# One order of work for four engines and two queues, written out by hand and drawn up anew

## The chip, the cores and the metric

The kernel runs on one core of one Trainium2 chip. The core has TensorE (PE; its weight loads are listed as PEld), VectorE (DVE), ScalarE (ACT), GpSimd (POOL) and SyncE (SP). Each of them works through its own instructions in the order in which they were emitted. SyncE and GpSimd issue the DMA transfers of this kernel, each through a queue of its own (q1 and q0 on the profile's page). The metric is the device time of one execution in microseconds (us).

## The reference

Two independent layers over a sequence of S = 2048 with D = 1024 channels, bf16; their results stand side by side in the output.

```python
# A: a short shift convolution (4 taps), a long convolution by FFT of length 2S, two gates
k_shift = sum over t of k_pad[:, t:t + S, :] * shift_k[:, ks - 1 - t]
kv = k_shift * v
y = irfft(rfft(kv padded to 2S) * rfft(ssm_k padded to 2S))[:S]
a = q * (y + kv * ssm_D)
# B: a diagonal state space layer with 1024 complex states
Bu = einsum("bld,pd->blp", x, B_bar)
h[t] = Lam_bar * h[t - 1] + Bu[t]
b = 2.0 * einsum("blp,dp->bld", hseq, Cmat).real + x * Dskip
return concatenate([a, b], -1)
```

## The kernel before

**The order is a string.** The whole kernel is emitted by one loop over the words of `ORDER` (L67 to L186, 1489 words). A word names a task, its arguments and the slots that it takes: `lh.15:a41` calls the function that `E` holds under `lh` with the argument 15 and gives it unit 41. `p` is one of 8 PSUM banks, `a` one of 53 units of 1024 elements a partition in one SBUF buffer (the arena; a task of several units takes neighbouring ones from the number on), `h` one of 3 slots for the scans' results (gslot), `w` one of 3 slots for constant matrices (wslot). The functions (L268 to L765) emit one task each. Since every engine and queue works in order of emission, the sequence of the words is the sequence of work on each of them. Where two tasks touch the same bytes of a slot, the later one waits for the earlier: a load into a unit waits until the last reader of that unit is done, also where this reader is a store that is still under way, and what stands behind the load on its queue waits with it.

**Layer A** is an FFT in two stages, both done by matrix products.

- `kp`, `vp` (L570 to L579) load rows of k and v; `kvm`, `kva`, `kvb`, `kvc` (L588 to L603, VectorE) do the shift convolution and the product with v.
- `am` (L608) is the first stage for kv, `ae` (L614) evicts it, `ast` (L617, GpSimd) stores it to a scratch in HBM. `hl` (L623) loads the long filter, `hT` (L632) transposes it on TensorE, `hc` and `hd` (L637 to L647) evict it, `hm` (L657), `he` (L665) and `hst` (L668) are its first stage.
- For each of 16 pairs of frequency groups, `lw` (L672) loads the pair's constant matrix into a wslot, `lh` and `lk` (L677) load the scratch rows of filter and kv, `sh` and `sk` (L688) are the second stage, `she` (L697) and `ske` (L704) evict it, `sw` (L708, GpSimd) or `swp` (L708, SyncE) swaps partitions by a transfer, `pr` (L714, VectorE) multiplies the spectra, `sa` (L726) is the way back, `sae` (L734) evicts it and `vst` (L737, GpSimd) stores it.
- `vl` (L742) loads that in the other order, `qp` (L747) loads q, `a3` (L754) is the last stage, `a3e` (L761) evicts it, `qm` (VectorE) multiplies by q, and `ost` (L764, GpSimd) or `osp` (L765, SyncE) stores the output.

**Layer B** runs in 16 blocks of 128 steps.

- The head: small tables of the parameters (`ld_par`, `par_T` L279, `p32` L284, `dve2`, `sin0` and others), `wb` and `wbe` (L402, L408) for the shift taps; `bl`, `bT`, `bc` (L415 to L431) load, transpose and evict B; `cl`, `cT`, `cx`, `cc` (L435 to L439) do the same for C; `dd` (L371, VectorE) makes diagonal matrices of Dskip.
- Each block: `x` (L447, SyncE) loads x transposed, `U` (L464) multiplies it by B, `ue` (L473) evicts, `r1` and `r3` (L487), `r2` (L498), `cy` (L500), `sc` (L504, the scan itself) and `r4` (L510) are VectorE's and ScalarE's part, `y` (L520, L523) or `yq` (L538) multiplies by C, `ye` (L556) evicts, and `ysh`, `ysp` (SyncE), `ysg`, `yst` (GpSimd) store (L560 to L564).

An eviction is a copy from PSUM. Its word without a `v` is ScalarE's, with a `v` (`a3ev`, `saev`, `bcv`) VectorE's:

```python
    def either(nm, f):
        E[nm] = lambda *a: f(nc.scalar.copy, *a)
        E[nm + "v"] = lambda *a: f(nc.vector.tensor_copy, *a)
```

Of the kernel before, what the change touches and what calls it, by code (L numbers as in the profile page):

```python
# [72 lines left out]
bT.2.1:p0 U.0.0.1 bT.3.0:p7 bc.5.0 bc.2.1 bc.5.1 kva.3 kring U.1.2.0:p5 bl.3.1:a23 cl.0.0:a14 bT.2.0:p2 bT.3.1:p0
bl.7.1:a46 ue.1.0:a34 U.0.2.1:p6 bc.3.1 bc.2.0 U.0.2.0 U.1.2.1 cl.3.0:a37 bl.7.0:a26 cl.1.0:a25 bT.7.1:p2 kvb.3:a22
bT.7.0:p0 ue.0.0:a23 bc.6.1 kp.-2 x.3:a21 U.0.1.0:p3 bc.3.0 gz stt cl.2.0:a12 cT.0.0:p4 bc.7.0 bc.7.1 U.0.1.1 U.0.3.0:p0
kvm.1:a15 ue.1.2 vp.1:a27 U.0.3.1 U.3.2.0:p1 ue.0.1 U.3.0.0:p3 z1 kvm.2:a42 z2 ld_Q U.1.1.1:p2 ue.0.2 ue.0.3 x.2:a52
U.1.1.0 cl.3.1:a13 kva.1 cT.1.0:p7 cl.2.1:a32 kva.2 kvb.1:a14 kvb.2:a39 ue.1.1 kvm.0:a15 rta kvc.3 U.3.0.1 cx.6.0 kva.0
cc.1.0 am.3.1:p0p6 cl.1.1:a51 U.3.1.1:p2 ue.3.0:a44 ae.3.0.1:a19 cc.0.0 U.3.2.1 kvc.2 ue.3.2 am.3.0:p7p3 cT.3.1:p0
vp.0:a30 cc.3.1 cx.7.0 kvb.0:a29 U.3.1.0 ue.3.1 cT.1.1:p5 U.3.3.0:p4 r1.0:a46 ae.3.1.1 kvc.0 U.3.3.1 kp.2 am.2.1:p2p0
r2.0:h1 cc.1.1 ue.3.3 cl.0.1:a27 hl.0.1:a23 kvc.1 am.0.0:p5p6 ae.3.0.0 cT.2.1:p1 ae.2.1.1:a40 sc.0.0 hl.0.0 U.1.3.1:p4  # L80
ae.3.1.0 sc.0.1 U.1.3.0 am.0.1:p3p0 ae.0.1.0:a31 cc.2.1 ae.0.0.0 ae.0.0.1 ae.0.1.1 ae.2.0.1 cT.0.1:p7 U.2.0.1:p1
r1.3:a15 cc.0.1 ue.1.3 ast.0 U.2.0.0 am.1.1:p5p3 r3.0:a27 cx.5.0 U.2.3.0:p0 ae.1.0.1:a46 hl.1.0:a48 hl.1.1 ae.1.1.1
# [5 lines left out]
he.0.7.0.0:a50 y.0.0.3 hc.0.0:a13 hm.0.6.0:p4p2 ye.0.0:a19 hm.0.4.1:p5p7 y.0.1.0:p6 y.0.1.1 y.0.1.2 y.0.1.3 vp.2:a34
kvb.4:a31 he.0.6.0.0 sc.1.1 he.0.4.1.1 vp.3:a26 r1.2:a14 he.0.4.1.0 he.0.7.0.1 hst.0.7.0 r3.1:a46 hm.0.0.1:p1p5
hst.0.4.1 hc.0.5:a42 he.0.6.0.1 r4.1 hm.0.0.0:p2p3 he.0.0.1.0:a48 cy.2:h1 r2.2 hm.0.5.1:p7p0 ye.0.1 he.0.5.1.1:a23  # L90
he.0.5.1.0 kp.3 he.0.0.1.1 kvm.6:a38 he.0.0.0.0 y.1.1.0:p4 kvc.4 y.1.1.1 hst.0.6.0 hst.0.6.1 kp.4 kva.6 hst.0.5.1
hm.0.5.0:p6p0 he.0.5.0.0 kvm.5:a14 y.1.1.2 he.0.0.0.1 kvb.6:a25 he.0.5.0.1 y.1.1.3 hm.0.7.1:p2p7 ye.1.1:a28 he.0.7.1.0
# [5 lines left out]
kvb.7:a31 ysp.0 U.4.0.1 r3.2:a48 hT.1.6:p5 he.0.1.1.1 ast.6 ast.4 he.0.2.1.0 hT.1.5:p4 r4.2 he.0.2.0.1 kvc.7 hT.1.4:p6
U.4.2.1:p1 ue.4.1 ue.4.0 hc.1.6:a22 hc.1.4:a19 am.5.1:p7p0 hT.1.3:p2 U.4.2.0 hc.1.5:a33 hT.1.7:p3 am.5.0:p6p4
ae.5.0.1:a15 yst.1 cy.3 y.2.1.0:p7 kp.5 hT.1.1:p5 hst.0.2.0 hd.2 y.2.1.1 ae.5.1.0 hdv.3 ae.5.0.0 hc.1.7:a30 ae.5.1.1  # L100
hst.0.2.1 hT.1.2:p4 y.2.0.0:p6 ue.4.2 hc.1.1:a14 sc.3.1 sc.3.0 hT.1.0:p0 y.2.0.1 am.7.0:p3p1 hc.1.3:a18 hst.0.1.0
r3.3:a40 hm.1.7.1:p5p2 hc.1.0:a34 ae.7.1.0:a27 he.1.7.1.1:a25 hst.0.3.0 y.2.1.2 ae.7.0.0 hst.0.3.1 am.7.1:p2p1 ast.5
# [6 lines left out]
hm.1.5.1:p2p6 he.1.5.1.1:a51 he.1.5.1.0 hst.1.5.1 yq.3.6 yq.3.7 ye.3.1:a24 hm.1.5.0:p6p4 kvm.11:a28 he.1.2.0.1 hst.1.2.0  # L109
hm.1.0.1:p3p5 cy.4 he.1.5.0.0 kp.6 kvb.10:a33 U.5.1.1:p2 U.5.1.0 sc.4.0 U.6.3.0:p7 kva.11 sc.4.1 hst.1.3.1 ye.3.0  # L110
ue.5.1:a40 he.1.0.1.0:a17 U.5.3.1:p2 hm.1.0.0:p3p1 kvc.9 ast.8 he.1.5.0.1 hst.1.5.0 kvb.11:a46 hm.1.6.0:p0p6 he.1.0.0.0
he.1.0.0.1 he.1.6.0.1:a47 U.5.3.0 hst.1.2.1 hst.1.3.0 U.6.3.1 he.1.6.0.0 U.6.0.1:p1 hm.1.1.0:p6p0 ue.5.3 ysp.3
hm.1.1.1:p2p3 he.1.0.1.1 hm.1.6.1:p5p4 he.1.1.0.0:a22 U.6.0.0 r3.4:a42 he.1.6.1.0 kvm.13:a12 he.1.1.1.1 U.5.2.0:p6
ue.6.0 U.5.2.1 he.1.6.1.1 hst.1.6.1 r4.4 he.1.1.1.0 hst.1.1.1 U.7.0.0:p3 he.1.1.0.1 vp.5:a50 U.5.0.0:p0 hst.1.0.1
hst.1.0.0 kvc.10 am.9.0:p2p4 kvc.11 kva.13 U.7.0.1 ae.9.1.0:a29 kvm.15:a49 ae.9.0.0 ue.7.0:a24 U.5.0.1 U.7.3.0:p4 ue.5.0
am.9.1:p1p0 vp.7:a34 ae.9.0.1 x.10:a26 kvb.13:a17 U.7.3.1 vp.6:a42 am.10.0:p3p1 kvm.14:a18 kvm.12:a13 kva.15 yq.4.0:p5p2
yq.4.1 yq.4.2 yq.4.3 ae.10.0.0:a44 ae.10.1.0 ue.7.3 ae.9.1.1 am.11.1:p3p0 ue.5.2 U.7.1.0:p1 kvc.13 ue.6.3 am.10.1:p4p6
ae.10.1.1 hst.1.1.0 kva.12 U.7.1.1 kvb.15:a4 am.11.0:p6p7 cy.5:h1 yq.4.4 kva.14 kvc.15 ae.10.0.1 yq.4.5 ue.7.1 yq.4.6
yq.4.7 kvb.14:a32 x.8:a23 ae.11.0.1:a10 ae.11.1.1 hst.1.6.0 lh.0:a46 ae.11.1.0 ae.11.0.0 ye.4.0:a28 am.13.0:p3p1
am.13.1:p6p0 ye.4.1 ae.13.0.1:a48 ae.13.0.0 U.6.2.0:p7 lh.1:a8 U.6.2.1 U.7.2.1:p4 am.15.0:p6p2 ast.9 x.9:a52 kvb.12:a50  # L120
ae.13.1.0 ue.6.2 ae.13.1.1 ae.15.0.0:a19 U.7.2.0 kvc.14 ae.15.1.0 am.14.0:p7p3 ue.7.2 ae.14.0.0:a29 ae.14.1.0
am.15.1:p6p1 am.14.1:p2p5 ae.15.0.1 U.8.3.0:p7 ast.10 lw.0:w0 ast.13 r1.5:a15 kvc.12 am.12.0:p4p3 ast.11 r2.5 ae.14.0.1
# [720 lines left out]
```

## Time and profile before

| | before |
| --- | --- |
| device time, median of 3 runs | 343.81 us (343.48 to 343.87) |
| profiled execution, its span | 343.2 us |
| TensorE matmuls busy | 329.5 us |
| VectorE busy | 325.1 us |
| ScalarE busy | 273.5 us |
| GpSimd busy | 68.9 us |
| moved by DMA | 100.83 MB |

The profile is of one execution. Its span runs from the first to the last recorded instruction; the device time is a little longer. "Busy" is the time in which an engine works on an instruction that the profile counts; issuing transfers, waiting on semaphores and branching are not counted. A line of waits tells who sat idle, until what came; a row of the timeline tells the start, the duration, the engine, the line of the kernel, the operation with its tiles and, in brackets, the idle time before it. A DMA's row on SPq or POOL is its issue only; when it has landed stands in a row of its own.

### The profile page before, as it was taken

The numbers are of one execution on the slowest core, as the hardware profiler recorded it, in microseconds if no ns is written. First come the engines' busy times: TensorE is split into PE (matmuls) and PEld (weight loads), VectorE is DVE, ScalarE is ACT, GpSimd is POOL, SyncE is SP. The second block draws the span as 40 slices with busy tenths as digits, with TensorE's granted clock in tenths as the row PEclk, the third lists the DMA queues.
The fourth block names the chain that finished last, engine by engine and source line by source line (L and its number), as shares of the span: only waits on it lengthen the run. The fifth ranks groups of instructions, "written<-read, shape, count | busy, mean of one in ns | idle before, by whom it ended". The sixth has DMA issues, their size and how long they took to land.

```text
span 343.2 us, 11813 instructions
## 1 busy us (share of the span) xinstructions
PE 329.5 (96%) x5086; PEld 230.2 (67%) x5105; DVE 325.1 (95%) x263; ACT 273.5 (80%) x519; POOL 68.9 (20%) x111
## 2 busy tenths in 40 slices
PE   5799999999999999999999999999999999999993
...
DVE  4989999999999999999999999999989999999991
...
PEclk9999999999999999999999999999999999999998
...
GB/s 177 352 351 208 315 281 283 155 318 365 368 269 198 264 263 295 233 261 343 313 353 282 270 339 212 369 272 311 280 314 276 216 326 378 327 335 284 375 346 274
DMA packets 62592, 100.83 MB, mean 294 GB/s; under 512 B 29422, under 2 KB 31614, under 8 KB 62540
## 3 DMA queue, kind: packets, MB, share of 16 engines
...
## 4 chain that ended last, share of the span: by engine, by line
PE 74%; ACT 15%; DMA 4%; issue 3%; DVE 3%; SPq 0%; POOL 0%; DVEq 0%; POOLq 0%
PE bank L464 25%; PE bank L538 19%; PE bank L520 10%; PE bank L754 4%; PE bank L688 4%; PE bank L726 4%; PE bank L608 2%; PE bank L657 2%; ACT BT L431 2%; ACT arena L614 2%; ACT arena L473 2%; ACT CT L439 2%; ACT arena L637 2%; DMA wslot<-a_c_W 1%; DMA arena<-arena 1%
## 5 line engine op out<-in xcount | busy, mean ns | idle before, releaser
L464 PEld LDWEIGHTS <-BT 128*128 128x128 bf16 x2048 | 117.8, 98 | 14.4 <-issue 9.9
L464 PE MATMUL bank<-arena,BT 128*128 128x128 bf16 x2048 | 125.4, 221 | 1.1 <-ACT BT L431 0.9
L538 PE MATMUL bank<-CT,gslot 64*64 64x512 bf16 x1408 | 86.6, 378 | 0.0
L504 DVE TENSOR_TENSOR_SCAN gslot<-rtab,gslot 128x1040 bf16<-128x1040 f32 x32 | 73.0, 2311 | 0.5
L538 PEld LDWEIGHTS <-gslot 64*64 64x64 bf16 x1408 | 36.9, 107 | 30.8 <-issue 1.9
L473 ACT CAST arena<-bank 128x512 bf16<-128x512 f32 x63 | 40.5, 660 | 13.8 <-PE bank L464 13.4
L614 ACT CAST arena<-bank 128x512 bf16<-128x512 f32 x64 | 37.2, 680 | 6.7 <-PE bank L608 4.0
L697 ACT CAST arena<-bank 128x512 bf16<-128x512 f32 x63 | 35.0, 617 | 5.9 <-issue 2.8
L520 PE MATMUL bank<-CT,gslot 128*128 128x512 bf16 x153 | 38.5, 380 | 0.3
L665 ACT CAST arena<-bank 128x512 bf16<-128x512 f32 x64 | 35.2, 631 | 3.1 <-PE bank L657 3.0
L714 DVE TENSOR_TENSOR arena<-arena 128x4096 bf16<-128x4096 bf16 x16 | 36.5, 2280 | 1.1 <-DMA arena<-arena 1.0
L487 DVE TENSOR_TENSOR arena<-gslot,Z 128x4096 bf16<-128x4096 bf16 x16 | 36.6, 2287 | 0.8 <-DVE gslot L504 0.2
L704 ACT CAST arena<-bank 128x512 bf16<-128x512 f32 x60 | 34.4, 621 | 3.2 <-PE bank L688 3.0
L734 ACT CAST arena<-bank 128x512 bf16<-128x512 f32 x60 | 32.4, 616 | 5.5 <-PE bank L726 5.3
L487 DVE TENSOR_TENSOR arena<-arena,Z 128x4096 bf16<-128x4096 bf16 x16 | 36.5, 2280 | 0.1
L556 ACT CAST arena<-bank 128x512 bf16<-128x512 f32 x31 | 18.1, 599 | 16.6 <-PE bank L538 8.7
L588 DVE TENSOR_TENSOR arena<-arena 128x4096 bf16<-128x4096 bf16 (+3 forms) x16 | 30.0, 1881 | 0.0
L668 POOL DMA_DIRECT2D Ys_h<-arena x32 | 23.2, 735 | 25.5 <-ACT arena L665 20.2
L617 POOL DMA_DIRECT2D Ys_kv<-arena x16 | 11.2, 726 | 83.5 <-ACT arena L614 81.1
L520 PEld LDWEIGHTS <-gslot 128*128 128x128 bf16 x160 | 14.1, 98 | 15.9 <-issue 2.3
L688 PE MATMUL bank<-arena,wslot 64*64 64x512 bf16 x256 | 21.5, 382 | 0.3 <-DMA wslot<-a_c_W 0.3
L737 POOL DMA_DIRECT2D Vs<-arena x16 | 11.7, 731 | 46.3 <-ACT arena L734 41.3
...
## 6 DMA issues: line engine op xcount, KB each, us to landing
Ys_kv<-arena POOLq DMA_DIRECT2D x16, 512.0 KB, 5.6
...
arena<-Ys_h SPq DMA_DIRECT2D x16, 512.0 KB, 5.0
arena<-Ys_kv SPq DMA_DIRECT2D x16, 512.0 KB, 5.6
Vs<-arena POOLq DMA_DIRECT2D x16, 512.0 KB, 5.6
arena<-Vs SPq DMA_DIRECT2D x16, 512.0 KB, 6.7
...
arena<-in_A_k_dram SPq DMA_DIRECT2D x8, 512.0 KB, 5.2
```

What stands on the lines that cost most here:

```text
L464: nc.tensor.matmul(pu[:, w, jl, :], BT[:, 2 * jp + jl, w, d, :], xT[:, d, :], start=(d == 0), stop=(d == ND - 1))
L473: cp(st["u", i][:, :, 2 * jp:2 * jp + 2, :], st.pop(("pu", i, jp)))
L487: nc.vector.tensor_mul(m, s_, win(Z))
L504: nc.vector.tensor_tensor_scan(gf, rtab[:].rearrange("p j t -> p (j t)"), gf, 0.0, ALU.mult, ALU.add)
L520: nc.tensor.matmul(py, h[:, w, j, 2:GW], CT[:, j, w, dh * 512:(dh + 1) * 512], start=(j == 0 and w == 0), stop=False)
L538: mm = nc.tensor.matmul(st["py", i, dh][cols, cs(r)], lhs(dh, rows, c), rhs(dh, rows), start=first, stop=last)
L614: cp(st["ysb", n2][:, p, dh * 512:(dh + 1) * 512], st.pop(("pa", n2, p, dh)))
L665: cp(o, st.pop(("pb", hf, s, e, r)).rearrange("p (n c t) -> p n c t", n=2, c=2))
L688: nc.tensor.matmul(st["ps", nm, g, l][64 * dh:64 * dh + 64, :], st["w", i][rows, a * WC:a * WC + 64], st[nm, i][rows, a, dh * 512:(dh + 1) ...
L697: cp(st["hab", i][:, 0, a, l, :], st.pop(("ps", "h", g, l)))
L704: cp(st["x16", i][:, a, l, :], st.pop(("ps", "k", g, l)))
L714: nc.vector.tensor_mul(hab, st.pop(("x16", i)).rearrange("p a l d -> p (a l d)").unsqueeze(1).to_broadcast([P, 2, 2 * D]), hab)
```

## The change

Only `ORDER` is changed; every function stays. The string after holds the same 1489 words up to the engine letters, so the same work.

- Compute tasks come in another sequence, and nearly all slots have other numbers.
- The loads and stores on SyncE and GpSimd keep their sequence, but for the stores that change queue: `ysp.4`, `ysp.6`, `ysp.10`, `ysp.13` and `osp.7` go to GpSimd as `yst` and `ost`; `yst.5`, `yst.11`, `ysg.14.0`, `ysg.15.1` and `ost.1` go to SyncE as `ysp`, `ysh` and `osp`. `ld_Q` comes ahead of `gz`.
- Evictions that change engine: VectorE's `a3ev` go from 9 to 6, `saev` from 4 to 2, `skev` from 4 to 3, `shev` and `uev` from 1 to 2 each; VectorE evicts 16 tiles in place of 20.

The string's lines that matter below, of 120 on either side: the head, the lines with `hl.2.1`, `x.5` and `lh.15`, and the tail.

```diff
-ld_w:a22 wb.3:p3 ld_par wbe.3:a8 par_T:p4 wb.0:p5 wb.7:p1 p32 ld_F bl.1.0:a39 bl.0.1:a18 wb.5:p7 bl.6.0:a34 bl.4.1:a14
-exp1 dve2 wbe.0 dve3 wb.6:p2 wb.4:p3 wb.2:p0 sm_pre wbe.7 bl.0.0:a27 wbe.5 x.0:a38 wb.1:p7 wbe.6 exp2 kp.1:a0 bl.1.1:a21
...
-he.0.3.1.0:a36 kvc.6 y.1.0.1 he.0.3.1.1 hst.0.5.0 kvb.5:a12 sc.2.1 ae.4.1.0 he.0.3.0.1 kvm.7:a13 y.1.0.2 am.4.1:p1p7
-hl.3.0:a40 he.0.3.0.0 hm.0.1.0:p5p0 y.1.0.3 he.0.1.0.0:a38 am.6.1:p5p6 ae.4.1.1 U.4.3.1:p7 he.0.1.0.1 ae.6.0.1:a17
-hl.2.1:a44 U.4.3.0 kvc.5 ae.6.1.1 am.6.0:p6p5 U.4.0.0:p2 ae.4.0.1 ue.4.3:a23 U.4.1.1:p3 ae.6.0.0 hm.0.2.0:p0p6 ae.6.1.0
...
-hst.1.7.0 he.1.3.1.1 yq.3.3 hm.1.2.1:p7p6 x.6:a37 he.1.2.1.0:a19 kva.9 he.1.2.1.1 he.1.3.0.0 kvc.8 x.5:a36 lw.1:w2
-kvb.9:a35 kvm.10:a47 U.6.1.0:p3 U.6.1.1 am.8.1:p6p7 ast.7 hst.1.7.1 r1.4:a40 kva.10 ae.8.1.1:a44 hst.1.4.1 ae.8.0.1
-r2.4:h0 am.8.0:p5p2 ae.8.0.0 ae.8.1.0 hst.1.4.0 ue.6.1:a38 yq.3.4 yq.3.5 hm.1.2.0:p5p7 he.1.2.0.0 x.7:a27 kp.7
...
-ske.22.1 yq.10.1 yq.10.2 ske.18.0 sw.9.0 vst.8 ye.9.0 sa.15:p6p5 lh.15:a41 ske.23.0 cy.11:h0 pr.9 ske.23.1 sae.15.1:a50
-x.12:a52 swp.11.0 r1.11:a20 yq.10.3 sa.14:p7p3 sae.15.0 sae.14.0 sa.19:p5p4 lw.10:w0 sa.18:p6p1 lk.12:a16 r2.11 yq.10.4
-sae.18.0:a39 yq.10.5 sae.19.0 saev.19.1 sae.14.1 vst.7 yq.10.6 yq.10.7 sh.20:p6p7 sh.21:p3p4 she.20.0:a3 sae.18.1
...
-a3.7.1:p6 a3e.7.1 a3.7.0:p4 a3e.7.0 qm.2 qm.0 osp.0 osp.2 yst.12 a3e.15.1 a3.6.1:p3 a3ev.6.1 qm.3 y.15.1.1 y.15.1.2
-y.15.1.3 ysg.14.1 ost.3 ye.15.1:a1 ysg.15.1 y.15.0.0:p4 y.15.0.1 a3e.15.0 y.15.0.2 qm.7 osp.7 y.15.0.3 ye.15.0 ysh.15.0
+ld_w:a33 ld_par par_T:p1 p32 dd exp1 dve2 wb.5:p0 wbe.5:a8 wb.7:p1 wbe.7 ld_F wb.0:p2 wbe.0 dve3 tabA1:a40a50a47a29
+bl.1.0:a32 wb.4:p7 wbe.4 wb.1:p4 wbe.1 bT.1.0:p3 bc.1.0 wb.3:p5 bl.0.1:a12 sm_pre bl.6.0:a26 bl.4.1:a39 bl.0.0:a24
...
+ae.6.1.1 hm.0.1.1:p4p1 r4.2 he.0.1.1.0 he.0.1.1.1 U.4.0.0 hl.3.0:a39 hl.2.1:a44 kvc.7 U.4.1.0:p3 hst.0.7.1 hl.3.1 hl.2.0
...
+he.1.2.1.1 am.8.1:p3p2 ae.8.0.1:a12 he.1.3.1.1 am.8.0:p5p4 ae.8.1.0 ae.8.0.0 ae.8.1.1 kvb.9:a19 U.6.1.1 r1.4:a39 x.5:a36
...
+sae.15.0:a39 sae.15.1 sa.14:p7p1 sae.14.0 sa.19:p6p3 sae.19.1:a15 sa.18:p5p4 sae.18.0 yq.10.4 yq.10.5 yq.10.6 yq.10.7
+sae.14.1 sae.18.1 vst.8 lh.15:a42 x.12:a47 swp.11.0 pr.11 ye.10.0:a49 lw.10:w0 sh.20:p1p7 she.20.1:a32 sh.21:p4p5
...
+y.15.1.0:p7 y.15.1.1 y.15.1.2 y.15.1.3 y.15.0.2 y.15.0.3 ye.15.1:a38 ye.15.0 ysh.14.0 qp.3:a32 a3ev.7.0 qm.3 ost.5 qm.2
+osp.4 osp.1 osp.0 osp.2 yst.12 ysg.14.1 ost.3 ysh.15.1 qm.7 ost.7 ysh.15.0
```

Unit 44 in the new string is taken by `kvm.2` at the head and later by others, the last reader ahead of `hl.2.1` being `kvb.5`; unit 36's last reader ahead of `x.5` is `am.8.0`; unit 42 ahead of `lh.15` holds the result that `vst.8` stores.

More of the change, by code (lines that the diff above doesn't have):

```diff
@@ L73 @@
[L73 to L82, printed above, removed]
@@ L88 @@
[L88 to L92, printed above, removed]
@@ L98 @@
[L98 to L102, printed above, removed]
@@ L108 @@
-r2.4:h0 am.8.0:p5p2 ae.8.0.0 ae.8.1.0 hst.1.4.0 ue.6.1:a38 yq.3.4 yq.3.5 hm.1.2.0:p5p7 he.1.2.0.0 x.7:a27 kp.7
[L109 to L122, printed above, removed]
@@ L133 @@
-sh.5:p0p3 she.5.0:a32 yq.6.2 yst.5 she.4.1 yq.6.3 lw.5:w1 sk.5:p0p5 she.4.0 she.5.1 sa.1:p4p2 sa.0:p1p3 ske.5.0:a13
-sae.1.0:a8 yq.6.4 ske.5.1 sae.0.0 sae.1.1 yq.6.5 sae.0.1 sh.10:p4p5 she.10.1:a0 she.10.0 yq.6.6 sh.11:p5p0 she.11.0
-she.11.1 yq.6.7 swp.2.0 sk.4:p1p4 ske.4.1 r3.7:a42 r4.7 yq.7.0:p5p2 yq.7.1 ye.6.1:a21 lw.4:w0 sw.5.1 ske.4.0 ye.6.0
-x.14:a36 swp.2.1 cy.8:h2 sh.9:p3p0 yq.7.2 she.9.0:a48 sh.8:p7p1 lk.7:a46 swp.5.0 yq.7.3 vst.0 she.9.1 r1.8:a4 she.8.1
-she.8.0 lk.4:a40 sk.11:p0p3 ysp.6 ske.11.1:a28 sk.10:p4p6 pr.2 sa.5:p7p1 ske.10.0 ske.11.0 yq.7.4 ske.10.1 sa.4:p4p3
@@ L143 @@
-ske.12.0 x.11:a14 lk.8:a12 r2.9 yq.8.5 r1.10:a41 sh.17:p7p2 yst.7 sh.16:p4p6 vst.4 lh.7:a32 swp.6.0 yq.8.6 yq.8.7 vst.5
-sc.9.0 she.17.1:a6 sk.17:p2p3 she.16.0 she.16.1 sk.13:p5p6 swp.6.1 she.17.0 ye.8.1:a25 ye.8.0 U.11.0.1:p4 sc.9.1
-r3.9:a48 ske.13.1 U.11.0.0 ske.17.1:a16 ske.13.0 ue.11.0:a18 pr.6 sk.16:p7p0 lw.7:w0 sh.15:p1p6 sw.8.1 U.11.3.1:p5
-U.11.3.0 ske.16.1 she.15.1:a37 ske.17.0 she.15.0 sk.15:p2p0 sh.14:p3p6 ysp.8 ue.11.3 r4.9 U.11.1.1:p1 ske.16.0 U.11.1.0
-ske.15.0:a12 she.14.1 sa.12:p2p6 ske.15.1 she.14.0 swp.8.0 x.13:a31 sa.13:p0p4 ue.11.1 U.11.2.0:p7 cy.10:h2 sk.14:p3p1
@@ new lines @@
+wb.6:p0 wbe.6 x.0:a38 wb.2:p6 kp.1:a0 bT.0.1:p2 wbe.3 wbe.2 bc.0.1 bT.0.0:p0 bc.0.0 bl.1.1:a31 tabA2 exp2 sin0 par_rest
+sin1 kp.0 bT.6.0:p7 x.1:a33 kvm.3:a17 bT.4.1:p1 U.0.0.0:p6 bT.1.1:p0 bl.3.0:a42 sin2 eo bT.3.0:p3 bc.3.0 bl.5.1:a36
+bT.5.1:p4 bl.2.1:a45 bl.4.0:a32 bl.6.1:a12 U.1.0.0:p2 bc.4.1 bT.4.0:p5 bc.4.0 bl.5.0:a31 bl.2.0:a14 bcv.1.1 U.1.0.1
+ue.1.0:a34 kva.3 kp.-1 bT.2.0:p0 bc.5.1 bcv.6.0 bT.5.0:p7 bc.5.0 bl.3.1:a36 cl.0.0:a37 bT.2.1:p1 bc.2.1 kring bc.2.0
+kvb.3:a42 stt kvm.1:a15 kvm.2:a44 bl.7.1:a43 cl.3.0:a20 U.1.2.0:p5 bl.7.0:a14 U.0.0.1 ue.0.0:a31 kva.1 cl.1.0:a23
@@ new lines @@
+U.0.2.0:p4 kp.-2 kva.2 bT.3.1:p7 bc.3.1 z1 x.3:a52 kvm.0:a25 U.1.2.1 cl.2.0:a39 vp.1:a48 bT.7.1:p2 bc.7.1 bT.6.1:p6
+U.0.1.0:p3 bc.6.1 ld_Q kvb.2:a19 kvb.1:a12 kva.0 x.2:a21 bT.7.0:p0 bc.7.0 cl.3.1:a14 U.0.1.1 U.1.1.1:p7 U.3.2.1:p1
+ue.0.1 cl.2.1:a17 U.0.3.0:p6 cx.6.0 z2 U.0.2.1 ue.0.2 U.0.3.1 ue.0.3 ue.1.2 kvc.3 U.1.1.0 ue.1.1 U.3.3.0:p2 rta
+am.3.1:p6p3 cT.3.1:p7 ae.3.0.1:a46 kvb.0:a44 cl.1.1:a18 r1.0:a27 cc.3.1 am.3.0:p5p0 ae.3.0.0 U.3.0.0:p4 U.3.2.0
+ue.3.2:a13 kvc.2 gz r2.0:h1 vp.0:a15 cT.1.0:p7 kvc.0 ae.3.1.0 U.3.3.1 sc.0.0 ae.3.1.1 cx.7.0 cT.0.0:p6 sc.0.1 ue.3.3
```

161 lines of the change are left out of this document (100 added, 61 removed).

## The prediction

> **What bounds the kernel now.** I read the page's busy line and slices first, for an engine without slack.
>
> ```profile
> PE 329.5 (96%) x5086; PEld 230.2 (67%) x5105; DVE 325.1 (95%) x263; ACT 273.5 (80%) x519; POOL 68.9 (20%) x111
> ...
> PE   5799999999999999999999999999999999999993
> ...
> DVE  4989999999999999999999999999989999999991
> ...
> PEclk9999999999999999999999999999999999999998
> ...
> PE 74%; ACT 15%; DMA 4%; issue 3%; DVE 3%; SPq 0%; POOL 0%; DVEq 0%; POOLq 0%
> ```
>
> Two engines are full, TensorE (96%) and VectorE (95%), both short of ten tenths only in the first two and the last slice. The granted clock is full until the end. The chain, the last of these lines, is three quarters TensorE. Where the free time lies is told by the table by stretches; its columns are the stretch, its length, the busy time (and instructions) of PE, PEld, DVE, ACT and POOL, the clock, the DMA share and GB/s.
>
> ```profile
> 0.00:10.00 10.00, 6.28 (x33) 3.60 (x34) 4.96 (x16) 6.92 (x13) 5.62 (x17) 1.00 0.71 193
> 10.00:20.00 10.00, 8.00 (x76) 7.57 (x75) 8.66 (x22) 10.00 (x24) 0.00 (x0) 1.00 1.08 369
> 20.00:247.00 227.00, 224.65 (x3675) 160.61 (x3687) 224.59 (x167) 201.03 (x375) 47.93 (x70) 1.00 0.97 287
> 246.00:336.00 90.00, 89.45 (x1322) 57.93 (x1316) 87.19 (x62) 55.00 (x109) 15.03 (x25) 1.00 0.93 319
> 335.00:343.20 8.20, 3.05 (x18) 1.34 (x15) 1.23 (x1) 1.07 (x2) 1.27 (x2) 0.84 0.73 268
> ```
>
> From 20 to 247 us the idle time is 227.00 - 224.65 = 2.35 us on TensorE and 2.41 us on VectorE; from 246 to 336 it is 0.55 and 2.81 us. So up to 247 both engines are equally tight, and behind it TensorE alone decides: VectorE's 2.81 us of slack there costs nothing. The DMA share of 0.93 to 1.08 says that a load has no private road and lands when it lands. The waits say what the few stalls are (who waits, for what, us in total, times, longest).
>
> ```profile
> PEld L726 <- DVE arena L714: 1.5, 3, 0.8
> DVE arena L601 <- PE bank L415: 1.3, 1, 1.3
> PEld L538 <- DVE gslot L510: 0.5, 1, 0.5
> PE bank L688 <- DMA wslot<-a_c_W: 0.3, 1, 0.3
> PE bank L608 <- DVE arena L603: 0.3, 1, 0.3
> ```
>
> Of these, 1.5 + 0.5 + 0.3 = 2.3 us are TensorE waiting for VectorE, and 0.3 us is one wait for a load, that of `lw.10`. The chain from that load on:
>
> ```profile
> 117.68 3.68 PE bank L464 x64
> ...
> 242.26 4.99 DMA wslot<-a_c_W
> ...
> 247.92 3.68 PE bank L464 x64
> ...
> 338.09 0.58 ACT arena L556
> ```
>
> The load issued at 242.26 lands 4.99 us later, at 247.25, and what follows it on the chain is TensorE, without another transfer or VectorE step, until the last eviction at 338.09 and its store. The reader is to see a narrow gate at 247: what is late there is late at the end, since the stretch behind it holds 0.55 us of TensorE idle time in all.
>
> **The change part by part.** Both orders hold the same 1489 words of work, so no matmul, scan or load is added or removed; what changes is order, slots and some copies' engines. Laid over each other, the two orders have done the same amount of work on every engine within a microsecond or so at each landmark I compared (each `sc`, each `pr`, each `a3`). It is a reshuffle within the same plan, and I price what it does at places.
>
> *Copies that change engine.* Twenty PSUM evictions on VectorE become sixteen.
>
> ```profile
> L761 DVE CAST arena<-bank 128x512 bf16<-128x512 f32 x9 | 5.9, 679 | 0.0
> L761 ACT CAST arena<-bank 128x512 bf16<-128x512 f32 x23 | 12.4, 592 | 6.4 <-PE bank L754 4.5 <-PE bank L523 1.9
> ```
>
> VectorE loses 4 x 0.68 = 2.7 us and ScalarE gains 4 x 0.59 = 2.4 us. All of it lies behind 250 us, where ScalarE is busy 55.00 of 90 us and VectorE has slack already, and TensorE does not wait for either. I cost it at 0; the bounds are -2.7 us (if VectorE set the end there) and +0.6 us (one copy that TensorE waits for). The cover is TensorE's 89.45 of 90 us; without it the whole 2.7 us would come through.
>
> The Trainium skill, "Perfetto Trace Analysis", section "Identifying the Most-Contended Engine", holds the busy share of matmuls to be a bad measure and takes that of the weight loads. By it TensorE stands at 67%, VectorE at 95% would be the engine to relieve, and this part would be worth its full -2.7 us. The stretches from 20 us on speak against it: TensorE leaves hundredths of each stretch unused, and its waits for VectorE there add up to 2.3 us in all.
>
> *The head.* The 1.3 us in which VectorE waits in `kvb.3` for TensorE's transposes go, since work that needs nothing (`dd`, `rta`) comes ahead of them:
>
> ```profile
> L371 DVE TENSOR_SCALAR Dd<-ident,p 128x128 bf16<-128x128 bf16 x8 | 1.4, 246 | 0.0
> ```
>
> `dd` takes 1.4 us and now fills an earlier wait. Against it stand a wait of `par_rest` for a sine that ScalarE does later (I count 0.9 us), less an earlier start by 0.4 us. Net, VectorE is about 0.85 us further at 45 us (1.3 + 0.4 - 0.9), TensorE is 0 to 1.2 us behind there, by the work ahead of it. TensorE can profit only through its 2.3 us of waits for VectorE. I keep 0 and -0.85 as bounds.
>
> *Slots that make loads wait.* SyncE's words keep their sequence, but a load goes only when its slot's last reader is done, and everything behind it on that queue waits too. Eight loads now wait for something later than before. Five of them (`bl.5.0`, `bl.3.1`, `bl.7.0`, `cl.2.1`, `vp.0`) are wanted late enough, by 1 us or more, and cost 0. Two come close:
>
> ```profile
> 77.05 2.33 SPq L623 DMA_DIRECT2D arena<-in_A_ssm_k_dram  x4
> arena<-in_A_ssm_k_dram SPq DMA_DIRECT2D x4, 512.0 KB, 8.5
> 81.49 0.68 DVE L601 TENSOR_TENSOR arena<-arena 128x1024 bf16<-128x1024 bf16 x1
> 89.78 1.66 PE L632 MATMUL bank<-ident,arena 128*128 128x128 bf16 x24
> DMA to landing us min/median/max: 3.6/6.7/7.3
> ```
>
> `hl.2.1` (second of the four issues at 77.05) gets unit 44, which `kvb.5` reads until 81.49 + 0.68 = 82.17. Behind it are `hl.3.1`, `hl.2.0` and the store `ysp.0`. The last load goes at 82.17 + 2 x 0.58 = 83.3 and lands, with the median of 8.5 us, at 91.8. The transposes that want it (L632, three in the row at 89.78) come near 90.7 in the new order: a wait of 1.1 us. `x.5` gets unit 36, free when `am.8.0` ends near 112.1. The last row is the landing time of the transposing loads of L447: 115.7 to 119.4, at the median 118.8, against `U.5.1.0` near 117.68: 0 to 1.7 us, 1.1 at the median. Together 2.2 us of new waits on TensorE between 90 and 118. Behind them VectorE, not held by them, runs ahead, so the 2.3 us of later waits for it shrink by about as much. For head and these two loads together I take -0.2 us, near the upper one of its ends -0.85 and +0.5 (1.1 + 1.7 - 2.3), because TensorE has nearly no way to use VectorE's lead.
>
> *The load at the gate.* `lh.15` gets unit 42, which in the new order holds the data of the store `vst.8`. So it waits until that store has landed. Behind it on SyncE are `x.12`, `swp.11.0`, `lw.10`, `lk.12` and `lw.15`.
>
> ```profile
> 236.21 0.74 POOL L737 DMA_DIRECT2D Vs<-arena  x1
> Vs<-arena POOLq DMA_DIRECT2D x1, 512.0 KB, 4.9
> 237.66 0.85 SPq L677 DMA_DIRECT2D arena<-Ys_h  x1
> 238.60 1.73 SPq L447 DMA_TRANSPOSE arena<-in_B_x_dram  x1
> 240.38 0.57 SPq L708 DMA_DIRECT2D arena<-arena  x1
> 242.26 0.36 SPq L672 DMA_DIRECT2D wslot<-a_c_W  x1
> wslot<-a_c_W SPq DMA_DIRECT2D x1, 160.0 KB, 5.0
> wslot<-a_c_W SPq DMA_DIRECT2D x1, 160.0 KB, 2.7
> 246.56 0.39 PE L538 MATMUL bank<-CT,gslot 64*64 64x512 bf16 x4
> 247.29 0.62 PE L688 MATMUL bank<-arena,wslot 64*64 64x512 bf16 x8 [0.34 <-DMA wslot<-a_c_W]
> ```
>
> The first two rows: `vst.8` was issued at 236.21 and landed 4.9 us later, at 241.1. `lh.15` went at 237.66, 3.4 us before that. From `lh.15` to the end of `swp.11.0` SyncE took 240.38 + 0.57 - 237.66 = 3.3 us, so `lw.10` goes at 241.1 + 3.3 = 244.4 in place of 242.26, 2.1 us later. At 5.0 us (the first row of L672, this very load) it lands at 249.4; TensorE is free at 246.56 + 0.39 = 246.95 and waits 2.45 us where it waited 0.34: +2.1 us. At 2.7 us (the second, `lw.11` issued at 229.56) it lands at 247.1: a wait of 0.15, -0.2 us. If `vst.8` goes half a microsecond earlier, +1.6. I take **+1.6 us**, nearest to the load's own row.
>
> For the store the Trainium skill has a price, "DMA: Bandwidth & Descriptors", section "Anatomy of one DMA — SWDGE (gpsimd) path": a fixed 2.0 us and the bytes at 436 GB/s, by which 512 KB give an estimate of 3.2 us. The row has 4.9 us for this store beside busy queues. By the page `lw.10` would be 0.4 us late only, and the sum would come out near 344.0 us.
>
> *Stores between queues and the tail.* Five stores move from SyncE to GpSimd and five the other way. Each issue is 0.5 to 0.9 us on a queue with room (GpSimd is busy 20%). The last store is `ysh.15.0` on SyncE as before, so the tail of 343.2 - 338.09 = 5.1 us stays. Cost 0, bounds of one issue either way, +-0.7.
>
> **Sum.** 343.2 (span) + 0 (copies) - 0.2 (head and two loads) + 1.6 (gate) + 0 (stores) = 344.6 us of span. The device time lies 343.81 - 343.2 = 0.6 us above it (median of three runs, 343.48 to 343.87, against the profiled span), which gives **345.2 us**; its own range is 344.3 to 346.2.
>
> **Rivals.** *The gate opens in time (same).* `lw.10` is late at issue but lands in 2.7 us; the rest cancels: 343.8 - 0.2 - 0.2 = 343.4 us. For it: the 2.7 us row. Against: this load at this place took 5.0 us. The same time comes out if the new order doesn't do to the queue what I say, `vst.8` going 2 us or more earlier.
>
> *The head's lead comes through (faster).* The end of the chain turns when TensorE reaches 247 earlier than now and `lw.10` is there. It needs `lw.10` issued before 244.1 (at 2.7 us) or before 242 (at 5.0). Then VectorE's 0.85 us come through its 2.3 us of waits, and the 0.34 us of the gate go: 343.81 - 0.85 - 0.34 = 342.6 us. For it: most waits of TensorE before 247 are on VectorE. Against: the three loads with later slots.
>
> *VectorE bounds the end (faster).* The copies' 2.7 us come through: 342.6 - 2.7 = 339.9 us. Against it: 89.45 of 90 us.
>
> *Several loads late (slower).* If the waits at 91 and 118 are not made good, 1.1 + 1.1 us join the gate's: 343.81 + 1.6 + 2.2 = 347.6 us.
>
> **How the numbers follow.** Chances: forecast 0.38, the gate in time 0.25, the head's lead 0.25, VectorE's end 0.05, several loads late 0.07. About 0.2% (0.7 us) is what a measurement of this kernel can tell from no change: faster is below 343.1, slower above 344.5. Faster 0.25 + 0.05 = 0.30, same 0.25, slower 0.38 + 0.07 = 0.45. The range reaches from 341.9 (the head's lead and one issue's 0.7 us more) to 347.2 (the forecast's sum with the gate's full 2.1 us and 1.5 of the 2.2 us of late loads not made good), and leaves out VectorE's end and the worst of the late loads.
>
> **What would show it.** In the profile after: `lh.15` (L677) waiting on SyncE until the store of `vst.8` (L737) has landed, `lw.10` (L672) issued near 244, and TensorE at L688 waiting near 2 us for the slot around 247, which then stands on the chain; TensorE at L632 waiting near 91 and at L464 near 118 for loads; the wait of L601 for L415 gone; VectorE near 322 us busy. I am wrong if L688 doesn't wait, if TensorE waits elsewhere behind 247, or if the waits at 91 and 118 are far larger than 1 us each and reach the end.

## The result: slower by 0.7%, and the profile after

The kernel after takes 346.76 us (median of 6 runs, 344.55 to 347.11) beside 343.64 us of the kernel before in the same series; the ratio is 1.0066 with a 95% interval of 1.0038 to 1.0094, so about 2.3 us more. The medians alone are 3.1 us apart, a quotient of 1.009, so the size is known as 2 to 3 us only; the forecast was 345.2 us, with a range of 341.9 to 347.2. Ratios here leave out runs that lie far above the others of their kernel; one of the six of the kernel before is such a run, at 1574.9 us, and the median of its other five is 343.48 us. The profiled execution took 346.42 us, its span 344.7 us. The page after has the same two full engines:

```profile
PE 328.6 (95%) x5105; PEld 230.1 (67%) x5105; DVE 324.1 (94%) x259; ACT 275.3 (80%) x523; POOL 69.0 (20%) x111
...
PE   5779999999999899999999999999999999999993
...
DVE  5899999999999999999999999998999999999980
...
PE 80%; ACT 8%; DMA 7%; SPq 2%; issue 1%; POOL 0%
```

The chain, the last of these lines, now has 7% of DMA where it had 4%, and 2% of SyncE's own issuing where it had none. The table by stretches (columns as before: stretch, length, PE, PEld, DVE, ACT, POOL, clock, DMA share, GB/s) and the waits (who, for what, us in total, times, longest) say where:

```profile
0.00:10.00 10.00, 6.12 (x29) 2.85 (x30) 5.91 (x18) 6.82 (x12) 5.65 (x17) 1.00 0.69 166
10.00:20.00 10.00, 7.19 (x104) 6.56 (x102) 9.12 (x22) 9.93 (x24) 0.00 (x0) 1.00 1.08 376
20.00:247.00 227.00, 223.40 (x3644) 161.90 (x3648) 222.90 (x163) 200.75 (x376) 47.75 (x70) 1.00 0.95 283
246.00:336.00 90.00, 89.49 (x1347) 57.83 (x1340) 86.94 (x59) 57.65 (x115) 14.85 (x23) 1.00 0.95 325
```

```profile
PE bank L415 <- DMA arena<-in_B_B_re_dram: 2.8, 2, 2.2
...
PE bank L464 <- DMA arena<-in_B_x_dram: 1.1, 1, 1.1
...
PE bank L688 <- DMA wslot<-a_c_W: 0.5, 1, 0.5
```

From 20 to 247 us TensorE is busy 1.25 us less than before (223.40 against 224.65). It now waits for three transfers: B's rows in the head, `x.5`, and the constants of `lw.10`. The first isn't the new order's alone: the two variants of the kernel before that are profiled below wait 1.7 and 1.8 us for B's rows at L415. From 246 to 336 it is as full as before. In the chain of waits the new links stand in the order of time:

```profile
111.89 6.57 DMA arena<-in_B_x_dram
...
236.71 5.66 DMA Vs<-arena
...
245.03 3.54 DMA wslot<-a_c_W
```

`x.5` goes at 111.89 and takes 6.57 us. `vst.8` takes 5.66 us and lands at 242.37, and what stands behind it is SyncE's queue, in its timeline:

```profile
238.06 0.48 SPq L708 DMA_DIRECT2D arena<-arena  x1
242.38 0.36 SPq L677 DMA_DIRECT2D arena<-Ys_h  x1
242.79 1.51 SPq L447 DMA_TRANSPOSE arena<-in_B_x_dram  x1
244.36 0.57 SPq L708 DMA_DIRECT2D arena<-arena  x1
245.03 0.53 SPq L672 DMA_DIRECT2D wslot<-a_c_W  x1
```

SyncE stands still from 238.54 to 242.38, until the store has landed; then `lh.15`, `x.12`, `swp.11.0` and `lw.10` go one behind the other. That is the queue as the prediction had it; the wait at its end is 0.51 us and not 2.45.

To compare the kernels at equal work I use one number that isn't a row: the start of a TensorE task less the sum of the undisturbed durations of all its tasks ahead of it. The difference of two columns tells how far one kernel is behind the other when as much work is done (work and delay in us, each from one profiled execution; the variants are those of the next section).

```
work done   before   after   e3     e5     f1     f2
   24       10.90    11.20  11.39  11.23  11.12  11.48
   66       13.63    13.00  12.88  13.05  12.91  13.00
  100       14.75    14.40  14.19  14.43  14.24  14.39
  120       15.55    16.45  15.06  15.30  15.12  15.26
  214       20.11    20.96  18.81  19.05  18.87  19.48
  240       21.65    22.97  22.12  20.59  20.42  20.83
  262       22.73    24.08  23.24  23.66  21.67  22.35
  300       23.47    24.77  23.92  25.63  22.71  23.03
```

After against before: 0.6 us ahead at 66 (the head), 0.35 ahead at 100, 0.9 behind at 120 (`x.5`), and 1.3 behind at the end.

### The profile page after: what moved, and what is told of

Read it like the earlier page. It is cut to its first block, busy times and chain, and to the rows that moved or that the text cites. A ratio compares the mean times of both kernels' runs of the same rounds, so it can differ in the third digit from the quotient of the medians.

```text
span 344.7 us, 11799 instructions
## 1 busy us (share of the span) xinstructions
PE 328.6 (95%) x5105; PEld 230.1 (67%) x5105; DVE 324.1 (94%) x259; ACT 275.3 (80%) x523; POOL 69.0 (20%) x111
## 4 chain that ended last, share of the span: by engine, by line
PE 80%; ACT 8%; DMA 7%; SPq 2%; issue 1%; POOL 0%
PE bank L464 29%; PE bank L538 19%; PE bank L520 10%; PE bank L688 4%; PE bank L754 4%; PE bank L608 4%; PE bank L726 4%; ACT BT L431 3%; PE bank L632 2%; PE bank L657 2%; DMA arena<-in_B_x_dram 2%; DMA Vs<-arena 2%; DMA arena<-in_B_B_re_dram 2%; PE bank L415 1%; DMA arena<-arena 1%; DMA wslot<-a_c_W 1%
## 5 line engine op out<-in xcount | busy, mean ns | idle before, releaser
L464 PEld LDWEIGHTS <-BT 128*128 128x128 bf16 x2048 | 116.0, 98 | 15.1 <-issue 9.9
L464 PE MATMUL bank<-arena,BT 128*128 128x128 bf16 x2048 | 123.1, 219 | 1.5 <-DMA arena<-in_B_x_dram 1.1
L538 PEld LDWEIGHTS <-gslot 64*64 64x64 bf16 x1408 | 38.8, 107 | 28.3 <-issue 1.9
L473 ACT CAST arena<-bank 128x512 bf16<-128x512 f32 x62 | 38.3, 638 | 14.5 <-PE bank L464 14.5
L614 ACT CAST arena<-bank 128x512 bf16<-128x512 f32 x64 | 35.9, 644 | 5.0 <-PE bank L608 4.3
L734 ACT CAST arena<-bank 128x512 bf16<-128x512 f32 x62 | 33.3, 623 | 5.3 <-PE bank L726 3.3
L704 ACT CAST arena<-bank 128x512 bf16<-128x512 f32 x61 | 33.6, 626 | 3.5 <-PE bank L688 3.5
L697 ACT CAST arena<-bank 128x512 bf16<-128x512 f32 x62 | 34.2, 639 | 2.5 <-PE bank L688 2.4
L556 ACT CAST arena<-bank 128x512 bf16<-128x512 f32 x31 | 18.1, 599 | 21.5 <-PE bank L538 15.0
L665 ACT CAST arena<-bank 128x512 bf16<-128x512 f32 x64 | 34.0, 623 | 1.3 <-ACT arena L473 0.5
L688 PE MATMUL bank<-arena,wslot 64*64 64x512 bf16 x256 | 21.9, 382 | 0.8 <-DMA wslot<-a_c_W 0.5
```

The source lines that it names most:

```text
L464: nc.tensor.matmul(pu[:, w, jl, :], BT[:, 2 * jp + jl, w, d, :], xT[:, d, :], start=(d == 0), stop=(d == ND - 1))
L473: cp(st["u", i][:, :, 2 * jp:2 * jp + 2, :], st.pop(("pu", i, jp)))
L538: mm = nc.tensor.matmul(st["py", i, dh][cols, cs(r)], lhs(dh, rows, c), rhs(dh, rows), start=first, stop=last)
L614: cp(st["ysb", n2][:, p, dh * 512:(dh + 1) * 512], st.pop(("pa", n2, p, dh)))
L665: cp(o, st.pop(("pb", hf, s, e, r)).rearrange("p (n c t) -> p n c t", n=2, c=2))
L688: nc.tensor.matmul(st["ps", nm, g, l][64 * dh:64 * dh + 64, :], st["w", i][rows, a * WC:a * WC + 64], st[nm, i][rows, a, dh * 512:(dh + 1) ...
```

## The experiments

Each ratio is to the kernel before, run beside it on the same chip, where the median of before was 344.2 to 344.6 us (three chips in all). Where two experiments are compared, their intervals (+-0.2 to 0.35%) should be kept in mind.

**One slot for `lh.15`.**

```diff
-lh.15:a42
+lh.15:a24
```

> The kernel after with one slot changed: lh.15 takes unit 24, free since vst.4, in place of unit 42, which vst.8 still stores from. Queue theory: lh.15 goes right behind swp.11.1, near 238.6 us in place of 242.38; lw.10 is then held only by its wslot, which sa.14 leaves near 243.2, in place of 245.03, and lands by 248; the wait of L688 for the wslot (0.51 us) is gone or under 0.2, and the time is 0.4 to 0.6 us below that of the kernel after (346.8 us, ratio to before 1.0066). Rival, the order of the compute tasks itself costs the time: the wait goes, another takes its place before 250 us, and the time stays within 0.2 us.

Ratio 1.0086 (1.0056 to 1.0115): no gain. SyncE's timeline and the chain show why:

```profile
237.92 1.22 SPq L677 DMA_DIRECT2D arena<-Ys_h  x1
239.19 1.83 SPq L447 DMA_TRANSPOSE arena<-in_B_x_dram  x1
241.07 0.57 SPq L708 DMA_DIRECT2D arena<-arena  x1
242.49 0.35 SPq L672 DMA_DIRECT2D wslot<-a_c_W  x1
...
242.49 6.18 DMA wslot<-a_c_W
...
PE bank L688 <- DMA wslot<-a_c_W: 1.4, 1, 1.4
```

`lw.10` went 2.5 us earlier and took 6.18 us in place of 3.54: it landed at 248.67, where it had landed at 248.57. L688 waited 1.4 us, the last line, from the waits. Both theories fail here: the queue's wait was gone, and yet the same wait of L688 stayed and grew. What the load's issue gained, its trip lost. Ahead of it in the same queue the 512 KB of `lh.15`, `x.12` and 256 KB of `swp.11.0` were now under way. That alone doesn't explain 6.18 us: in the kernel before the same three went ahead of it at the same spacing (`lh.15` at 237.66, `lw.10` at 242.26), and the trip took 4.99 us.

**A slot that lets `x.5` go early.**

```diff
-kvb.8:a36
+kvb.8:a43
```

> The kernel after with one slot changed: the product kv of block 8 takes unit 43 in place of 36, so that x.5 needn't wait for am.8.0. Queue theory: x.5 goes near 103 us in place of 111.89 and lands by 111; the wait of L464 for it near 118 us (1.15 us) is gone, TensorE runs about 0.4 us ahead of the kernel before at 118 us, and the end comes 0.5 to 1.2 us earlier than in the kernel after. Rival: TensorE has to wait for VectorE a little later anyway, the lead is used up by 200 us, and the time stays within 0.2 us of the kernel after.

Ratio 1.0065 (1.0036 to 1.0094), the same as after. The wait of L464 near 118 us is gone and TensorE gets to the load of `lw.10` earlier. There the profile loses the whole lead and more in one wait (the chain, then the waits):

```profile
234.90 5.62 DMA Vs<-arena
...
240.53 0.36 SPq L677
...
243.48 5.39 DMA wslot<-a_c_W
...
PE bank L688 <- DMA wslot<-a_c_W: 2.7, 1, 2.7
```

This is the gate of the prediction in its full size. `vst.8` lands at 240.52, `lh.15` goes at 240.53, `lw.10` at 243.48; its trip takes 5.39 us (5.0 was forecast) and L688 waits 2.7 us (2.45 was). In the kernel after the same loads behind the same wait gave a trip of 3.54 us and a wait of 0.5.

**Both slots.**

```diff
-kvb.8:a36
+kvb.8:a43
-lh.15:a42
+lh.15:a24
```

> Both slots changed. Queue theory: the two gains add up, 1.0 to 1.7 us below the kernel after, which leaves at most 0.3% over the kernel before, or level with it. Rival, the order itself: at most 0.3 us below the kernel after, ratio to before 1.005 or more.

Ratio 1.0058 (1.0036 to 1.0081). At work 214 TensorE is 2.15 us ahead of the kernel after; at 240, 0.85 us are left. L688 waited 1.8 us for a load issued at 241.06 that took 6.65 us:

```profile
241.06 6.65 DMA wslot<-a_c_W
```

From here on the question was no longer when the load may go, but what lies ahead of it.

**`lh.15` behind `lw.10`,** with `x.5` free (first) and without (second).

```diff
-kvb.8:a36
+kvb.8:a43
-... vst.8 lh.15:a42 x.12:a47 swp.11.0 pr.11 ye.10.0:a49 lw.10:w0 sh.20:p1p7
+... vst.8 x.12:a47 swp.11.0 pr.11 ye.10.0:a49 lw.10:w0 lh.15:a24 sh.20:p1p7
```

> The kernel after with x.5 freed (kv of block 8 in unit 43) and lh.15 (512 KB, unit 24) moved on SyncE's queue from ahead of x.12, swp.11.0 and lw.10 to right behind lw.10. With both slots free but lh.15 still ahead, lw.10 was issued at 241.06 and took 6.65 us, so what lies ahead of it in the queue, not its issue, set the gate at 247. Theory of the data ahead: issued near 241 as well (its wslot is not free sooner), it takes 3 to 4 us, lands by 245, the wait of L688 (1.82 us there) falls below 0.3, and the time is 1.5 to 2 us below that with both slots free: ratio to before 0.999 to 1.002. Rival, all transfers share one bandwidth and the load lands near 247 whatever its place: ratio 1.005 or more.

> The same move of lh.15, with x.5 still waiting for am.8.0. Theory of the data ahead: no wait at 247, but TensorE gets there 1.2 us later, so 1.0 to 1.4 us above the kernel with both; against the kernel after 0.5 us less: ratio 1.003 to 1.006. Rival, leads ahead of 247 don't reach the end: within 0.3 us of the kernel with x.5 freed too.

Ratios 1.0042 (1.0020 to 1.0064) and 1.0082 (1.0051 to 1.0113). `lw.10`, issued at 241.31 in the first, was waited for no more near 247 us in either: in the table the first has no step from 214 to 240 beyond that of before, and is 2.4 us ahead of the kernel after. Then it loses all of it, in two waits that the kernel after doesn't have:

```profile
PE bank L688 <- DMA wslot<-a_c_W: 1.8, 1, 1.8
...
PE bank L754 <- DMA arena<-Vs: 1.1, 1, 1.1
```

The first of them, at 271 us, is the load `lw.13`. SyncE's timeline ahead of it:

```profile
261.80 0.33 SPq L672 DMA_DIRECT2D wslot<-a_c_W  x1
265.61 0.36 SPq L677 DMA_DIRECT2D arena<-Ys_h  x1
266.14 1.24 SPq L447 DMA_TRANSPOSE arena<-in_B_x_dram  x1
267.47 0.54 SPq L708 DMA_DIRECT2D arena<-arena  x1
268.10 1.03 SPq L672 DMA_DIRECT2D wslot<-a_c_W  x1
```

It is the same figure once more: `lh.13` has the unit from which `vst.9` stores, and goes at 265.61 when that has landed (265.59); behind it stand `x.15`, `swp.12.1` and `lw.13`. In the kernel before `lh.13` waits for the multiply `sa.30` instead, but that lets it go no earlier (265.51). What differs is when TensorE asks for `lw.13` (the first two lines are the kernel before, its SyncE and its TensorE; the third is the variant):

```profile
267.94 0.59 SPq L672 DMA_DIRECT2D wslot<-a_c_W  x1
...
274.20 0.63 PE L688 MATMUL bank<-arena,wslot 64*64 64x512 bf16 x8
...
273.27 0.63 PE L688 MATMUL bank<-arena,wslot 64*64 64x512 bf16 x8 [1.76 <-DMA wslot<-a_c_W]
```

The load is issued at 267.94 there and at 268.10 here; the kernel before uses it at 274.20, the variant wants it at 271.51: the new order asks for it after 1.8 us less of TensorE's work, and the variant is 1 us ahead.

**The mirror in the kernel before:** `lh.15` behind `lw.10`, and `lh.15` made to wait for `vst.8`.

```diff
-lh.15:a41 ... lw.10:w0
+... lw.10:w0 lh.15:a41
```

> The kernel before with lh.15 moved right behind lw.10. Theory of the data ahead: its wait of 0.34 us at L688 goes, 0.1 to 0.4 us below the kernel before, ratio 0.999 to 1.000. Rival: lh.15 itself or sh.30, which wants it, becomes late near 252, ratio above 1.001.

```diff
-lh.15:a41
+lh.15:a1
```

> The kernel before with lh.15 in unit 1, so that it waits for vst.8 as in the kernel after, and nothing else. By the prediction lw.10 goes near 244.4 in place of 242.26, L688 waits 1.6 to 2.4 us in place of 0.34, and the time is 1.2 to 2.1 us above before: ratio 1.0035 to 1.006. Theory of the data ahead: issued late, lw.10 travels faster (3.5 us, as in the kernel after) and the wait is 0.6 to 1.2 us: ratio 1.001 to 1.0025.

The first: 1.0001 (0.9979 to 1.0023), no wait at L688 in its profile, and nothing to be gained. The second: 1.0057 (1.0021 to 1.0092), the size that the prediction gave this wait, and a wide spread, 344.44 to 351.52 us over all twelve runs. Its profiled run was one of the shortest (344.87 us); there `vst.8` had landed early enough for `lh.15` to go at 239.21, and L688 waited twice 0.3 us only. So one slot alone costs the kernel before half a per cent, but no profile here shows the longer runs of this variant in which it does.

**The third place, `lh.13`,** with the two others mended, and alone.

```diff
-lh.13:a15
+lh.13:a32
```

> The kernel after with three places mended: kv of block 8 in unit 43 (x.5 needn't wait), lh.15 behind lw.10, and now lh.13 in unit 32, free since sa.21, in place of 15, from which vst.9 still stores. With the first two alone TensorE was 2.4 us ahead of the kernel after at 247 us and lost it in a wait for lw.13 at 271 (1.76 us) and one for a load of Vs at 308 (1.11 us). Gates in series: lh.13 goes near 262 in place of 265.6, lw.13 near 265 in place of 268.1, the wait at 271 falls below 0.4 us and 1.3 to 1.8 us more reach the end: 344.3 to 345.0 us beside a kernel before of 344.5, ratio 0.999 to 1.0015. Rival, the last gate, the loads of Vs (L742) that wait for all of the stores: they go no earlier, the wait at 308 grows by what is won at 271, and the ratio stays 1.003 or more.

> The kernel after with only lh.13 in unit 32. Gates in series: in the kernel after TensorE comes to 271 us too late to wait there, so an earlier lw.13 gains nothing: within 0.3 us of the kernel after, ratio 1.006 to 1.009. Rival, each late load has a price of its own: 0.5 us or more below the kernel after.

Alone: 1.0075 (1.0049 to 1.0102), nothing won, as expected of gates in series. All three: 1.0048 (1.0020 to 1.0077), not the 0.999 to 1.0015 that was expected, although its profile shows all three waits gone and TensorE 0.75 us ahead of the kernel before at the end (table, f1). That profile is of the fastest of its twelve runs (343.79 us; the median is 345.89), so it doesn't show what the others wait for. What it does show is a wait too small to matter there:

```profile
304.40 1.46 PE L754 MATMUL bank<-arena,Gt 128*128 128x512 bf16 x5
306.04 0.61 PE L754 MATMUL bank<-arena,Gt 128*128 128x512 bf16 x2 [0.18 <-DMA arena<-Vs]
```

The last stage begins with the results 12, 3 and 5, which are the third, fifth and sixth of the loads of Vs, while the kernel before begins with 13, 12 and 1, the second to fourth. In this profile the second to fourth load landed at 300.45, 301.81 and 303.12, 1.3 to 1.4 us apart; by that step the fifth and sixth come at about 304.5 and 305.8, and TensorE starts on them at 304.83 and 306.04, on the second after a wait of 0.18. There is next to no slack. In five of the nine profiles of the order after and its variants (the one with the evictions changed apart) L754 waits 0.6 us or more, in none of the order before (the expectation below says six of eight).

**The loads in the sequence in which they are wanted.**

```diff
-vl.2:a16 ... vl.13:a4 vl.12:a10 ... vl.1:a20 vl.3:a1 ... vl.5:a51
+vl.12:a10 ... vl.3:a1 vl.5:a51 ... vl.2:a16 vl.13:a4 ... vl.1:a20
```

> The kernel with three places mended, and the first six loads of Vs (L742) in the sequence 12, 3, 5, 2, 13, 1 in place of 2, 13, 12, 1, 3, 5. The last stage (L754) asks for 12, 3 and 5 first, which are the third, fifth and sixth to be loaded; the kernel before asks for 13, 12 and 1, its second to fourth. In six of eight profiles of the order after and its variants TensorE waits at L754 near 305 to 309 us (0.5 to 3.6 us), in no profile of the order before. Theory that this last gate is what keeps the timed runs 1.4 us above before though no wait is seen in the one profile: ratio 0.997 to 1.001, with no wait of L754 above 0.2 us. Rival, the loss lies elsewhere (the head's loads of B, or the spread of landing times at all gates): ratio 1.003 to 1.006 as without the change.

Ratio 1.0003 (0.9984 to 1.0021), median 344.10 beside 344.20 us, and all twelve runs within 343.54 to 345.28. The profiled run is a plain one (344.46 us). Its first loads of Vs were issued late, from 296.57 on where those of the profile before this were from 293.74, and still L754 doesn't wait:

```profile
296.57 6.04 SPq L742 DMA_DIRECT2D arena<-Vs  x9
...
305.08 1.89 PE L754 MATMUL bank<-arena,Gt 128*128 128x512 bf16 x7
```

So this sequence was worth 0.45% of the 0.48% that were left (by the two intervals +-0.35%). It was changed only together with the three slots: what it brings alone in the kernel after, or costs in the kernel before, wasn't run.

**The stores back on their queues.**

```diff
-yst.4 yst.6 yst.10 yst.13 ost.7 ysp.5 ysp.11 ysh.14.0 osp.1 ysh.15.1
+ysp.4 ysp.6 ysp.10 ysp.13 osp.7 yst.5 yst.11 ysg.14.0 ost.1 ysg.15.1
```

> The kernel after with its ten moved stores on the queues that they had before (ysp.4, 6, 10, 13, osp.7 on SyncE; yst.5, 11, ysg.14.0, ysg.15.1, ost.1 on GpSimd), each at its place in the order of after. Theory that the stores cost at the end: from the last store's landing to the end of the span is 1.56 us in the kernel after and 1.04 before, and the device time lies 1.7 us above the span; both come back to before's, 0.5 us of the span and up to 1.1 us outside it, and the time is 0.5 to 1.5 us below the kernel after. Rival, stores hide: within 0.3 us of the kernel after.

Ratio 1.0098 (1.0064 to 1.0132): not faster. The profiled run, the slowest of its six (350.0 us), waits at the last gate:

```profile
PE bank L754 <- DMA arena<-Vs: 3.6, 1, 3.6
```

The premise of this experiment was wrong: the kernel before, too, takes 1.7 to 1.9 us more than its span in every run beside these experiments (344.25 and 342.5 us, for one).

**The evictions back on their engines.**

```diff
-a3ev saev skev shev uev yev of the order after (16 on VectorE)
+the 20 of the order before, each word at its place in the order after
```

> The kernel after with the twenty evictions that VectorE had before given back to it (and its own sixteen new ones that were ScalarE's before given to ScalarE), order and slots as after. The prediction: nothing, within 0.3 us of the kernel after, since TensorE leaves no room behind 247 us. Rival, VectorE bounds the end and the four copies fewer were worth up to 2.7 us: 1 to 2.7 us slower than the kernel after.

Ratio 1.0881 (1.0847 to 1.0916), 375.16 us, far outside of both expectations. VectorE now sits idle for matmuls of L688, at 256.15 ahead of a multiply and at 260.19 ahead of one of its copies; TensorE waits for a copy of VectorE's (L734):

```profile
256.15 2.29 DVE L487 TENSOR_TENSOR arena<-gslot,Z 128x4096 bf16<-128x4096 bf16 x1 [2.33 <-PE bank L688]
260.19 0.69 DVE L704 CAST arena<-bank 128x512 bf16<-128x512 f32 x1 [1.75 <-PE bank L688]
```

```profile
304.24 2.00 PE L464 MATMUL bank<-arena,BT 128*128 128x128 bf16 x24 [2.71 <-DVE arena L734]
```

An eviction's engine and its place in the order belong together; 24 words on the other engine at places chosen for this one cost 28 us. It says nothing on what four copies less on VectorE are worth, so that stays open.

## Why the prediction was right, and where it wasn't

The time lies in the forecast's range and moved the way that was forecast, for loads that come late. The size of the step, 2 to 3 us where 1.4 was forecast, and its split over the terms did not come out, and the largest part that the runs found was in no term. That the number fits is luck in part.

- **The bound.** Right that TensorE is dense from 247 us to the end in the profile before. Wrong to read from it that the gate at 247 is the last one. In the new order there are two more, `lw.13` at 271 and the loads of Vs at 305 to 309 us. They aren't seen in the profile after. For `lw.13` that fits with TensorE coming late there. For the loads of Vs it isn't enough: with the slot of `lh.15` changed alone TensorE starts L754 as late (306.92 us, 306.82 in the kernel after) and waits 0.6 us.
- **TensorE's waits for VectorE, 2.3 us.** Misread: 1.5 and 0.5 us of it are rows of PEld, the weight loads, which overlap with matmuls. The matmuls' own rows in the profile before have 0.3 us at L608 and the one below, so the room in which late loads could vanish, or VectorE's lead come through, was near 0.6 us by these rows:

```profile
PE bank L726 <- DVE arena L714: 0.3, 1, 0.3
```

- **The load at the gate, +1.6 us.** The mechanism holds step by step: `lh.15` waited for `vst.8` (242.38 where 241.1 was forecast), `lw.10` went at 245.03 (244.4). The size fails in the profile after: I took the trip of 5.0 us from before; it took 3.54 us, and TensorE itself came 1.15 us later, so the wait grew by 0.17 us. Why the trip was short isn't shown, since the variant with `x.5` free has 5.39 us behind the same queue. In the six profiles of the new order with `lh.15` ahead of `lw.10`, L688 waits 0.5, 1.4, 2.7, 1.8, 0.8 and 0.8 us, 1.0 us more on average than before. Two of the six (1.4 and 1.8 us) have the slot free, so the store is not all of it. The same slot put into the kernel before did cost 0.57%. The price that the Trainium skill, "DMA: Bandwidth & Descriptors", section "Anatomy of one DMA — SWDGE (gpsimd) path", gives for such a store (an estimate of 3.2 us) was not seen: `vst.8` took 5.66 us.
- **`x.5`, 1.1 us.** Right: issued at 111.89 (112.1), landed at 118.46 (118.8), a wait of 1.1 us. I let later waits for VectorE swallow it. In the profile after they took 0.6 us of it by work 168, but 0.85 us are lacking again at 214; at 201.5 us TensorE sits idle for 0.36 us there, and the profile names nothing that it waits for. Three other profiles that wait for `x.5` don't have this idle time and are level with the kernel before at 214, within 0.15 us by the same measure. Over the three pairs of variants that differ in `x.5` alone (1.0066 and 1.0065, 1.0086 and 1.0058, 1.0082 and 1.0042), freeing it brings 0.23% on average, some 0.8 us; one of the three shows nothing.
- **`hl.2.1`, 1.1 us.** Didn't come: its loads went from 81.04 us on and not 82.17, and no L632 waits.
- **The head.** TensorE is 0.6 us ahead at work 66, within the bounds (0 to 0.85) and more than I took; that this is VectorE's lead is inferred. That B's rows come late there (2.8 us of waits at L415) I had not seen; it is made good by work 66.
- **Copies, 0.** VectorE is busy 324.1 us and not near 322, the sign that I had named. What four copies less are worth stays open.
- **Stores and tail, 0.** Nothing here speaks against it for the stores themselves (1.0098 with them back). But no term asks in which sequence L754 wants its loads of Vs, which the new order changed, and that sequence was worth 0.45% (1.0048 to 1.0003). That missing term is what failed most.
- **The step from span to device time, 0.6 us.** It is 1.7 to 1.9 us in every run that lists both. So the profiled execution of before, 343.2 us of span, took about 344.9 us by that, 1.1 us over its median: the run was not a typical one. In the sum this cancels, since 343.2 + 0.6 is the median of 343.81 us again; the forecast is that median and 1.4 us.

With the three slots and the sequence mended the new order is level with the old one. That the order of the compute tasks itself brings anything isn't shown: at best one profile is 0.75 us ahead. What the longer runs of the variant with three slots mended wait for is inferred from the cure, not seen.
